# Two requests moved in a fused recurrence and router kernel: ranks one step later, a weight load behind a mask

## The chip, the cores and the metric

The kernel runs on one core of a Trainium2 chip. Its time is the device time of one execution in microseconds (us); the figure given is a median over several runs. A core has a matrix engine (PE, whose weight loads are shown as PEld), a vector engine (DVE), an activation engine (ACT), a general engine (POOL), and SP, which here only asks for transfers. Transfers (DMA) that SP asks for share one queue, q1; the indirect scatters and gathers that POOL asks for have another, q0.

## What is computed

The reference is a gated linear recurrence followed by a router with one expert for each token. The shapes are 4 batches, 8 heads, 768 positions and 48 channels a head; then 3072 tokens of 384 channels, 8 experts, 1024 hidden channels, all float32.

```python
for t in range(S):                                   # recurrence, state is D x D for each head
    state = alpha[:, :, t, :, None] * state + k[:, :, t] (x) v[:, :, t]
    y[:, :, t] = q[:, :, t] @ state
x = y as (B*S, H*D)                                  # 3072 x 384
logits = normalized(x) @ normalized(expert_emb).T / tau
e = argmax(logits);  gate = softmax(logits)[e]
out[token] = gate * (relu(x[token] @ w1[e]) @ w2[e])
```

## The kernel before

**Stage one: 24 chunks in steps.** The tokens are worked in `NS` = 24 chunks of 128 positions, 6 to a batch. A loop over `s` from 0 to 26 is a software pipeline written out by hand: step `s` works on several chunks at once. It loads chunk `s + 2` (`load`, SP: alpha in two parts, k and q; and v of chunk `s + 1`), turns chunk `s` and makes its decays (`decays`: PE transposes into `pa`, `pk`, `pq`, then a DVE scan `r` at L477 and the product `kr`; `decay_queries`: a second DVE scan `a` at L506 and the product `qs` on POOL at L510), makes the scores of chunk `s - 1` (`scores`: PE, then a mask on DVE at L577 for one half of the heads and, after a copy by ACT, on POOL by `affine_select` at L579 for the other half; that POOL instruction is kept as `st[s]["masked"]`), mixes chunk `s - 2` and turns chunk `s - 3` into rows of tokens with their logits (`rows`, L649 to L653).

The order on PE is written out: every block of matmuls stands in `with in_turn()`, which puts it behind the last matmul so far. On POOL a step's scatters stand `behind(s)`, behind the `qs` product of that step. On the other engines, SP among them, the order is that of the program except where the build puts an instruction that is ready earlier ahead of one that is not.

**Routing inside the pipeline.** The chunks are routed in groups (`GROUPS`): 0-3, 4-7, 8-11, 12-13, 14-15, 16-19, 20-22 and 23. When the last chunk of a group has its rows, `choose(g)` finds each token's expert on DVE and adds up how many tokens each expert had before each chunk (`before[:, s + 1]`, L340; on POOL, but on DVE for chunks 15 and 23). Some steps later `place(g)` makes each token's rank within its expert with two PE matmuls (three for the groups that end at chunk 15 and 23, which also need the totals), read by DVE at L362 to L369. From then on the group's chunks stand in the list `send`, and each step sends one of them, or two when more than two are waiting, to DRAM, sorted by expert: `to_rows`, an indirect scatter from POOL at L311 into `xs`.

How many steps later `place` comes is set at L690:

```python
late = 2 if s1 > NS - 3 else 3 if s1 == S0 else 4
placed_at.setdefault(s1 + late, []).append(g)
```

`s1` is the chunk after the group's last, and `S0` = 16. The group that ends at chunk 15 is therefore placed in step 19, the others in the step `s1 + 4`, but for the last two.

**The early start.** After 16 chunks at least one expert is sure to have 256 tokens. `first_expert` (DVE, L375 to L389) takes the first such expert from the totals of chunk 0 to 15 and writes the order in which the experts are worked (`turn_i`) and their first rows (`row0`). When chunk 15 has been sent, `fetch_early` (SP, L177 to L181) asks for that expert's first 256 rows out of `xs`, into `exg`; it waits for all the scatters before it. `weights(0)` (SP, L137 to L144; `w1` at L141, `w2` at L144, 1.5 MB each) is asked for in step 22, behind the last load of v. `weights(1)`, for the second expert, is asked for in step 23. From step 24 on, `turn_early` transposes the gathered rows on PE (into `pxe`, L194) and `first_layer_early` multiplies them by the first expert's `w1` (into `phe`, L191), between the last steps of stage one. All of this is in the chain `in_turn`: the rest of step 24 on PE stands behind `turn_early`.

**Stage two: the experts.** After the loop the counts of each expert are made (`counts`), rows of padding are scattered (`to_rows(pads[...], blank)`), and `fetch(0)` and `fetch(1)` ask SP for the rows of the first two experts (L170). Then the early rows go through the second layer, and the experts are worked in turn by `run(i)`, with `weights(i + 2)` and `fetch(i + 2)` asked for one iteration ahead. The first readers of the second expert's weights are `mix_first(1)` (DVE, L1009) and `mix_weights` (POOL, L979).

Of the kernel before, what the change touches and what calls it, by code (L numbers as in the profile page):

```python
# [27 lines left out]
def kernel(  # L28
# [12 lines left out]
    nc = tc.nc  # L41
# [8 lines left out]
    NS = N // P  # L50
# [15 lines left out]
    S0, EARLY = 16, 2  # L66
# [63 lines left out]
    w1_s = [consts.tile([P, KT, F], FP32, name=f"w1_{i}") for i in range(NW - 1)]  # L130
# [4 lines left out]
    def weights(i):  # L135

        e = nc.values_load(  # L137
            turn_i[0:1, i : i + 1], engines=(SP,), min_val=0, max_val=E - 1,
            skip_runtime_bounds_check_because="a sum of two experts, less E from E on",
        )  # L140
        nc.sync.dma_start(  # L141
            out=w1_s[i % NW], in_=w1_r[ds(e, 1)].rearrange("e p k f -> (e p) k f")
        )
        nc.sync.dma_start(  # L144
            out=w2_s[i % NW], in_=w2_r[ds(e, 1)].rearrange("e p k d -> (e p) k d")
        )
# [49 lines left out]
    def in_turn():  # L196
        return tc.issue_after(last["pe"].ins) if last else ExitStack()


    with ExitStack() as c1:  # L200
# [226 lines left out]
        st = [dict() for _ in range(NS)]  # L427
# [16 lines left out]
        def load(s):  # L444

            if s < NS:
                b, c = divmod(s, NCH)
                i = s % NBUF
                for p0, p1 in ((1, AROW), (AROW, P)):
                    nc.sync.dma_start(out=at_s[i][p0:p1, :, 0:D], in_=a_r[b, c, p0:p1])  # L450
                nc.sync.dma_start(out=kt_s[i][:, :, 0:D], in_=k_r[b, c])
                nc.sync.dma_start(out=qt_s[i][:, :, 0:D], in_=q_r[b, c])
            if s > 0:
                b, c = divmod(s - 1, NCH)
                return nc.sync.dma_start(out=vt_s[(s - 1) % NBV][:, :, 0:D], in_=v_r[b, c])
# [8 lines left out]
        def decays(s):  # L464

            d = st[s]
            i = s % NBUF
            L = NP * P
            pa = turned(at_s[i], "pa")
            r = r_s[s % NR]
            nc.vector.tensor_tensor_scan(  # L477
                r[:, L - 2 :: -1], pa[:, L - 1 : 0 : -1], inr[:, L - 2 :: -1],
                1.0, ALU.mult, ALU.add,
            )  # L480
            pk = turned(kt_s[i], "pk")
            d["kr"] = kr = work.tile([P, NP, P], FP32, name="kr", bufs=3)
            krf = kr.rearrange("p n t -> p (n t)")
            nc.vector.tensor_tensor(krf, pk, r, ALU.mult)
            d["pq"] = turned(qt_s[i], "pq")
            d["a"] = pa, r

        def queries(s, copied):

            d = st[s]  # L490
            d["qc"] = qc = work.tile([P, NP * P], FP32, name="qc")
            with tc.issue_after(copied.ins) if copied else ExitStack():
                nc.scalar.copy(qc, d["pq"])
# [24 lines left out]
        def keys_back(s, ps=ps_tr, tag="tr"):  # L518

            if s % NCH == NCH - 1 or "kb" in st[s]:  # L520
                return
            kr = st[s]["kr"]
            pkb = ps.tile([P, NP * P], FP32, tag=tag, name="pkb")
            for p in range(NP):
                tr(pkb[:, p * P : (p + 1) * P], kr[:, p], ident)
            st[s]["kb"] = kb = work.tile([P, NP * P], FP32, name="kb")
            nc.scalar.copy(kb, pkb)
# [135 lines left out]
        def turn_early():  # L663
            for t in range(EARLY):
                px = ps_tr.tile([P, KT, P], FP32, tag="tr", name="pxe")
                for k in range(KT):
                    tr(px[:, k], exg[:, t, k * P : (k + 1) * P], ident)
                nc.scalar.copy(exT[:, :, t * P : (t + 1) * P], px)
# [18 lines left out]
        send = []  # L687
        placed_at = {}
        for g, (_, s1) in enumerate(GROUPS):
            late = 2 if s1 > NS - 3 else 3 if s1 == S0 else 4  # L690
            placed_at.setdefault(s1 + late, []).append(g)

        def rows_of(s):
# [4 lines left out]
        def placing(s):  # L698

            n = None  # L700
            for g in placed_at.get(s, ()):
                r = GROUPS[g][1] - 1
                with in_turn():
                    n = place(g, r in (S0 - 1, NS - 1))
                if r == S0 - 1:
                    lead.append(n)
            return n
# [8 lines left out]
        for s in range(NS + 3):  # L716
            if s + 2 <= NS:
                v_last = load(s + 2)
            if s + 2 == NS:

                with tc.issue_after(v_last.ins):
                    weights(0)
            if 0 <= s - 1 < NS:
                with in_turn():
                    keys_back(s - 1)
            if s < NS:
                decays(s)
            if s == NS:
                with in_turn():
                    turn_early()  # L730
            copied = None
            if s < NS:
                placing(s)
            if 3 <= s <= NS:
                with in_turn():
                    copied = rows(s - 3)
            if s < NS:
                queries(s, copied)
                decay_queries(s)
            if 0 <= s - 1 < NS:  # L740
                decay_state(s - 1)

                with in_turn(), tc.issue_after(st[s]["a_scan"].ins) if s < NS else ExitStack():
                    scores(s - 1)
            if s == 0:
                with behind(s), in_turn():
                    prepare_first(a0)
                with behind(s):
                    prepare_logits()
            if NS <= s < NS + 2:  # L750
                with in_turn():
                    first_layer_early(2 * (s - NS), 2 * (s - NS) + 1)
            if 0 <= s - 2 < NS:
                with in_turn():
                    mix_states(s - 2)
                with in_turn():
                    mix_chunk(s - 2)
            if 0 <= s - 1 < NS:

                with in_turn(), tc.issue_after(st[s]["a_scan"].ins) if s < NS else ExitStack():  # L760
                    update(s - 1)
            if 0 < s < NS and s % NCH == 0:

                with in_turn():
                    keys_back(s, ps_mm, "mm")
            if NS <= s < NS + 2:
                with in_turn():
                    first_layer_early(2 * (s - NS) + 1, 2 * (s - NS) + 2)
            if NS <= s < NS + 2:
                with in_turn():  # L770
                    rows(s - 2)
            if s == 1:
                with in_turn():
                    turn_logits()
            if s == 2:
                with behind(s):
                    routing_constants()
            if s == 3:
                with behind(s):
                    convert_constants()  # L780
            if 4 <= s < 4 + NXG * (NC + 1):
                i, t = divmod(s - 4, NC + 1)
                with behind(s):
                    nc.gpsimd.memset(xg_s[i][:, t], 0.0)
            if s == 3:
                with behind(s):
                    nc.gpsimd.memset(blank, 0.0)

            if s >= NS:
                n = placing(s)  # L790
            if lead:
                with behind(s):
                    first_expert(lead.pop())
            with behind(s) if s < NS else tc.issue_after(st[NS - 1]["masked"].ins):
                n_now = len(send) if s >= NS else 0 if s == NS - 1 else 1 + (len(send) > 2)
                for c in send[:n_now]:
                    to_rows(dest[:, c : c + 1], x_g[group_of[c]][:, c - GROUPS[group_of[c]][0]])
                    send.remove(c)
                    if c == S0 - 1:
                        fetch_early()  # L800
            if s == NS - 1:
                weights(1)
            for r in rows_of(s):
                g = group_of[r]
                if r == GROUPS[g][1] - 1:
                    choose(g)
                    with behind(s) if s < NS else ExitStack():
                        nc.gpsimd.tensor_copy(x_g[g][:, :, TK], toks[:, slice(*GROUPS[g])])
            if s > NS:
                with in_turn():  # L810
                    first_layer_early(2 * (s - NS) + 2, 2 * (s - NS) + 4)
# [487 lines left out]
```

## Time and profile before

| | |
|---|---|
| median of 4 runs | 419.69 us (416.64 to 420.84) |
| profiled execution, its own time | 418.16 us |
| its span, first to last instruction | 416.5 us |
| busy: PE, PEld, DVE, ACT, POOL | 399.3, 354.0, 272.0, 177.7, 190.0 us |
| DMA queue q1 (SP), share of 16 engines | 49.14 MB, 50.1% |
| granted PE clock, mean | 0.996 |
| stage one, to the last matmul of `phe` | about 158 us |

A line of a timeline has the start of a run of like instructions in us from the start of the span, their time together, the engine, the line of the kernel, the operation, the tiles (written <- read), the shapes, the count, and in brackets how long the engine stood idle before it and what ended that idle time. A line of waits has the engine and what it would do, then what it waited for, and the sum, the number and the longest of these waits in us. A line of the table of windows has the window, its length, the busy time of PE, PEld, DVE, ACT and POOL with the number of instructions, the granted PE clock, the busy share of the DMA engines and GB/s. L191 and L194 are lines of helpers through which most matmuls and transposes of stage one go, so these are told apart by their tiles.

### The profile page before, as it was taken

The page shows a single profiled execution, that of the slowest core. Times are in us where ns is not written, and L with a number is a line of the kernel's source. Part 1 is how long each engine was busy: PE and PEld are TensorE (multiplying, and loading weights), DVE is VectorE, ACT ScalarE, POOL GpSimd, SP SyncE. Part 2 cuts the span into 40 slices and gives each one's busy share as a digit, 9 for nine tenths or more (in the row PEclk, how much of TensorE's full clock was granted, in tenths as well). Part 3 has the DMA queues.
Part 4 walks back from the last instruction along what each step waited for, and adds up shares of the span by engine and source line. Part 5 has one row for each costly group of instructions (what it writes and reads, how often), then busy time and mean ns, then how long its engine had stood idle before and what let it go on. Part 6 is the DMA issues. An engine that isn't in the chain of part 4 may idle for free. (4 is left out here: it accounts for less than half of the span.)

```text
span 416.5 us, 12218 instructions
## 1 busy us (share of the span) xinstructions
PE 399.3 (96%) x4730; PEld 354.0 (85%) x4730; DVE 272.0 (65%) x725; ACT 177.7 (43%) x478; POOL 190.0 (46%) x283
## 2 busy tenths in 40 slices
PE   7899999999899989999999999999999999999992
PEld 6788989889788776879799799799889979979982
DVE  7998989799798334715855945934762684684531
ACT  4455554645455426453523524522541362362310
POOL 7555586878575277308027027025203703603501
PEclk9999999999999999999999999999999999999998
DMA  9999999999998964959008119018204601001001
GB/s 140 156 162 153 156 193 181 202 169 181 195 205 221 392 221 138 308 185 350 2 35 326 67 44 352 26 52 299 76 19 162 241 2 58 2 0 55 0 18 43
DMA packets 119378, 60.25 MB, mean 145 GB/s; under 512 B 102287, under 2 KB 113816, under 8 KB 119312
## 3 DMA queue, kind: packets, MB, share of 16 engines
q1 hardware_dynamic: 115208, 49.14, 50.1%
q0 software_dynamic: 3728, 10.16, 7.0%
q8 instruction: 44, 0.72, 0.8%
q14 instruction: 22, 0.18, 0.2%
q10 hardware_dynamic: 376, 0.05, 0.1%
HBM read 49.69 MB, written 11.45 MB: 147 GB/s over the span
## 5 line engine op out<-in xcount | busy, mean ns | idle before, releaser
L850 POOL DMA_INDIRECT out_dram<-y,sx x25 | 24.3, 971 | 158.0 <-DVE gsh L906 77.4
L1032 PE MATMUL pq<-xT,w 128*128 128x192 f32 x280 | 64.5, 329 | 0.6
L955 DVE TENSOR_TENSOR hT<-pq,v 128x192 f32<-128x192 f32 x84 | 30.0, 357 | 33.5 <-PE pq L1032 31.7
L1032 PEld LDWEIGHTS pq<-xT,w 128*128 128x128 f32 x280 | 47.3, 190 | 2.8 <-DVEq L1198 1.7
L510 POOL TENSOR_TENSOR qs<-qc,a 128x512 f32<-128x512 f32 x24 | 30.6, 1276 | 34.9 <-DVE a L506 23.7
L939 PE MATMUL pyo<-w,hT 128*128 128x384 f32 x128 | 43.3, 492 | 0.0
L939 PEld LDWEIGHTS pyo<-w,hT 128*128 128x128 f32 x128 | 23.8, 190 | 15.3
L1032 PE MATMUL pq<-xT_m,w_m 128*128 128x192 f32 x168 | 36.5, 326 | 0.0
L1040 ACT ACTIVATE hT<-hT 128x384 f32<-128x384 f32 (+1 forms) x56 | 24.8, 443 | 23.0 <-DVE hT L955 19.9
L477 DVE TENSOR_TENSOR_SCAN r<-pa,inr 128x511 f32<-128x511 f32 x24 | 29.1, 1215 | 6.7 <-PE pa L194 6.5
L506 DVE TENSOR_TENSOR_SCAN a<-pa,ini 128x512 f32<-128x512 f32 x24 | 29.3, 1222 | 1.0
L1080 PE MATMUL pq<-w_m,hT_m 128*128 128x192 f32 x168 | 29.6, 326 | 0.0
L311 POOL DMA_INDIRECT xs<-x,dest x24 | 24.2, 1009 | 11.3 <-DVE x L653 6.2
L979 POOL TENSOR_TENSOR w_m<-w 128x384 f32<-128x384 f32 x28 | 27.4, 998 | 3.7 <-DMA out_dram<-y,sx 2.7
L1032 PEld LDWEIGHTS pq<-xT_m,w_m 128*128 128x128 f32 x168 | 28.9, 190 | 0.0
L1040 ACT ACTIVATE hT<-pq 128x192 f32<-128x192 f32 x28 | 9.2, 330 | 43.5 <-PE pq L1032 43.5
L1080 PEld LDWEIGHTS pq<-w_m,hT_m 128*128 128x128 f32 x168 | 27.7, 190 | 0.0
L979 POOL TENSOR_TENSOR w_m<-w,w_m 128x384 f32<-128x384 f32 x28 | 27.1, 996 | 0.0
L191 PE MATMUL sc<-qs,kr 64*64 64x128 f32 x768 | 26.3, 271 | 0.5 <-issue 0.5
L191 PE MATMUL pyx<-sm,vt 128*64 128x128 f32 x384 | 26.7, 279 | 0.0
L955 DVE TENSOR_TENSOR v<-pq,v 128x192 f32<-128x192 f32 x56 | 20.0, 356 | 8.4 <-ACT v L1043 5.2
L1087 DVE SCALAR_TENSOR_TENSOR y<-pq,gt,u 128x192 f32<-128x192 f32 x21 | 8.8, 418 | 24.6 <-PE pq L1080 24.6
(203 smaller groups left out, 932.0 us busy)
## 6 DMA issues: line engine op xcount, KB each, us to landing
w<-in_moe_w_dram SPq DMA_DIRECT2D x16, 1536.0 KB, 7.7
kt<-in_k_dram SPq DMA_DIRECT2D x24, 192.0 KB, 3.8
qt<-in_q_dram SPq DMA_DIRECT2D x24, 192.0 KB, 5.7
vt<-in_v_dram SPq DMA_DIRECT2D x24, 192.0 KB, 5.5
xg<-xs SPq DMA_DIRECT2D x22, 196.5 KB, 7.1
at<-in_alpha_dram SPq DMA_DIRECT2D x24, 168.0 KB, 5.2
xg<-xs SPq DMA_DIRECT2D x8, 98.2 KB
at<-in_alpha_dram SPq DMA_DIRECT2D x24, 22.5 KB, 4.3
```

What stands on the lines that cost most here:

```text
L191: last["pe"] = nc.tensor.matmul(*args, **kwargs)
L311: ins = nc.gpsimd.indirect_dma_start(out=xs, out_offset=bass.IndirectOffsetOnAxis(ap=rows, axis=0), in_=x, in_offset=None, bounds_check=E ...
L477: nc.vector.tensor_tensor_scan(r[:, L - 2 :: -1], pa[:, L - 1 : 0 : -1], inr[:, L - 2 :: -1], 1.0, ALU.mult, ALU.add,)
L506: d["a_scan"] = by_dve = nc.vector.tensor_tensor_scan(a, pa, ini, 0.0, ALU.mult, ALU.add)
L510: by_pool = nc.gpsimd.tensor_tensor(qs.rearrange("p n t -> p (n t)"), d["qc"], a, ALU.mult)
L850: ins = nc.gpsimd.indirect_dma_start(out=out, out_offset=bass.IndirectOffsetOnAxis(ap=col, axis=0), in_=y, in_offset=None, bounds_check=N - 1,
L939: pe[:] = [nc.tensor.matmul(py, lhsT=hT[:, f], rhs=w2_t[:, f], start=(f == 0), stop=(f == FT - 1),)]
L955: dve[:] = [call(*args)]
L979: nc.gpsimd.tensor_tensor(to[:, f], x[:, f], y[:, f], ALU.subtract)
L1032: pe[:] = [nc.tensor.matmul(to, lhsT=left, rhs=right, start=start, stop=stop, skip_group_check=True,)]
L1040: return nc.scalar.activation(h, p, AF.Relu)
L1080: pe[:] = [nc.tensor.matmul(to, lhsT=left[:, f], rhs=right[:, f], start=start and f == 0, stop=stop and f == n - 1, skip_group_check=True,)]
```

## The change

The group of chunks 14 and 15 loses its special case and is placed in step 20 instead of 19. With it move its two scatters in the list `send`, `first_expert`, and `fetch_early`, which follows chunk 15's scatter: that goes out in step 21 instead of 20.

`weights(1)` is written in step 24 instead of 23. Ahead of it one column of its `w1` tile is set to zero on POOL, behind the mask of the last chunk; the load of `w1` overwrites that column and so has to wait for it.

```diff
@@ -687,7 +687,7 @@
         send = []
         placed_at = {}
         for g, (_, s1) in enumerate(GROUPS):
-            late = 2 if s1 > NS - 3 else 3 if s1 == S0 else 4
+            late = 2 if s1 > NS - 3 else 4
             placed_at.setdefault(s1 + late, []).append(g)
 
         def rows_of(s):
@@ -798,7 +798,9 @@
                     send.remove(c)
                     if c == S0 - 1:
                         fetch_early()
-            if s == NS - 1:
+            if s == NS:
+                with tc.issue_after(st[NS - 1]["masked"].ins):
+                    nc.gpsimd.memset(w1_s[1][:, 0, 0:1], 0.0)
                 weights(1)
             for r in rows_of(s):
                 g = group_of[r]
```

## The prediction

> **What bounds the kernel now.** I read the page first: the busy shares, then the chain that ended last.
>
> ```profile
> PE 399.3 (96%) x4730; PEld 354.0 (85%) x4730; DVE 272.0 (65%) x725; ACT 177.7 (43%) x478; POOL 190.0 (46%) x283
> ```
>
> PE is busy for 399.3 of 416.5 us: a delay of PE anywhere is a delay of the end, because nothing behind it has spare time, and a gain is worth what PE waits less. The diff touches steps 19 to 24 (about 106 to 143 us). The waits from 104 to 124 us, longest first:
>
> ```profile
> DVE before L340 <- POOL before L340: 2.0, 1, 2.0
> ...
> PE pyx L191 <- POOL before L340: 1.5, 1, 1.5
> ...
> PE pq L194 <- DMA qt<-in_q_dram: 0.5, 1, 0.5
> ```
>
> They sit in step 19. From one step's first transpose (of `pa`) to the next one's is 5.3 us, but 8.5 us from step 19 to step 20 (105.98 to 114.52). PE stops at the rank matmuls; the timeline of PE has them, and the two places of step 24 that matter below:
>
> ```profile
> 109.67 0.40 PE L191 MATMUL pyx<-before,ones 128*128 128x16 f32 x2 [1.52 <-POOL before L340]
> ...
> 136.24 0.87 PE L194 MATMUL pxe<-ident,xg 128*128 128x128 f32 x6
> ...
> 139.44 1.56 PE L191 MATMUL phe<-exT,w 128*128 128x256 f32 x6
> ```
>
> `pxe` is the first reader of the early rows (the gather, `fetch_early`), `phe` of the first expert's `w1`. DVE's timeline over the same steps shows who really holds step 19:
>
> ```profile
> 109.65 0.17 DVE L340 TENSOR_TENSOR before<-before,chosen 128x8 f32<-128x8 f32 x1 [2.04 <-POOL before L340]
> 109.73 1.21 DVE L477 TENSOR_TENSOR_SCAN r<-pa,inr 128x511 f32<-128x511 f32 x1
> ...
> 125.39 0.42 DVE L560 TENSOR_TENSOR state<-pd,dec 128x256 f32<-128x256 f32 x1 [0.18 <-PE pd L191]
> 126.33 1.22 DVE L477 TENSOR_TENSOR_SCAN r<-pa,inr 128x511 f32<-128x511 f32 x1 [0.52 <-PE pa L194]
> ```
>
> DVE stands 2.04 us in its own addition at L340, which `choose` makes in step 18 and the change leaves there. Step 19's scan starts right behind it. From 109.73 to 122.3 DVE has no gap.
>
> Last, SP's queue, which asks for the gather and the weights, and POOL, whose scatters the gather waits for:
>
> ```profile
> 124.03 3.18 SPq L455 DMA_DIRECT2D vt<-in_v_dram  x2
> 128.62 0.40 SPq L181 DMA_DIRECT2D xg<-xs  x1
> 129.55 1.31 SPq L141 DMA_DIRECT2D w<-in_moe_w_dram  x1
> 131.04 0.37 SPq L144 DMA_DIRECT2D w<-in_moe_w_dram  x1
> 131.92 1.84 SPq L141 DMA_DIRECT2D w<-in_moe_w_dram  x1
> ```
>
> ```profile
> 121.67 1.01 POOL L311 DMA_INDIRECT xs<-x,dest  x1 [0.15 <-issue]
> ...
> 124.59 1.28 POOL L510 TENSOR_TENSOR qs<-qc,a 128x512 f32<-128x512 f32 x1 [0.52 <-DVE a L506]
> ```
>
> The scatter at 121.67 is chunk 15's, the last that the gather needs; the list of DMA issues gives it 4.3 us to landing (126.0). SP is busy with the loads until 127.21 and asks for the gather at 128.62, so today the gather isn't late. `fetch_early` is written in step 20, ahead of the loads that end at 127.21, yet stands behind them: the build lets SP's transfers that are ready sooner go first.
>
> **The change part by part.** *Ranks in step 20.* The matmuls (0.77 us of PE, 109.67 to 110.44), three DVE operations at L362 to L369 (0.2 us each at most) and `first_expert` (L375 to L389, about 2.1 us of DVE, 113.45 to 115.42 and 0.3 more) go one step on; nothing is saved. PE's 1.52 us wait goes, as the ranks' operands are then long there. What is late next is DVE: behind its 2.04 us it has the same operations to do between 109.73 and the scan of step 21 at 121.09, in another order and without a gap, so that scan does not move. What can shrink are DVE's later waits for a PE that is now ahead, 0.18 and 0.52 us. Bounds 0 to 0.7 us; with step 21's transposes of PE some 0.9 us earlier, and PE held again by the `a` scan whose bank it reuses, I take a gain of 0.4 at `pxe`: 135.8.
>
> *Scatters of chunks 14 and 15, and the gather.* `send` now holds 13 in step 19, 14 in step 20 and 15 in step 21: three scatters as before, one a step, about 1 us of POOL each, hidden in POOL's idle 1 to 2 us a step. Chunk 15's follows the `qs` product of 124.59, at 125.9, and lands 4.3 to 5.1 us later (chunk 15 and chunk 14 of today), at 130.3 to 131.1. SP is free at 127.21 and can't ask for the gather before then. The weights of the first expert need only `turn_i` (some 120 us) and the last load before them. If SP takes them first, it asks for `w1` 0.55 us after 127.21 (as it takes 0.53 us from the gather's issue to `w1`'s today), at 127.75, which is 1.8 us sooner than 129.55. The packets of the trace run through this one queue in the order asked: the gather's rows until 131.75, `w1` until 136.7, `w2` until 140.7. 1.8 us sooner, `w2` ends at 138.9. Then the gather's 0.40 MB: 1.0 us at the 401 to 422 GB/s of the windows from 133 to 136 us, or 2.2 us as it took on its own, and up to 0.7 us from last packet to landing (131.75 to 132.43). It lands at 140.3 to 141.6; I take 141.0. PE's order is chained by hand, so everything of step 24 stands behind `pxe`: 141.0 instead of 136.24 is **+4.8 us** (4.1 to 5.4), the 0.4 swallowed.
>
> *The clock behind such a gap.* PE would be idle 5.2 us, and no gap of this trace after the start is over 1.52 us. The nearest rows are at its ends. The last matmul ends at 409.1:
>
> ```profile
> 412.00:413.00 1.00, 0.00 (x0) 0.00 (x0) 0.00 (x0) 0.00 (x0) 0.00 (x0) 1.00 0.32 120
> 413.00:414.00 1.00, 0.00 (x0) 0.00 (x0) 0.00 (x0) 0.00 (x0) 0.00 (x0) 0.53 0.03 5
> ```
>
> The granted clock falls to half 4.0 us after it; and at the start a group of four transposes takes 1.06 us until 6.9 us, 5.3 us behind the first matmul (1.55), and 0.6 us later. So the price is between 0 (no fall) and 2.65 us (half of 5.3); I take **1.0**, as part of slower matmuls hides in the waits of ACT and DVE in that step.
>
> [...]
>
> *Second expert's weights behind the mask.* New is a memset of 128x1 on POOL; the nearest rows are 0.43 us (128x393, L784) and 0.21 (an addition of 128x8), so 0 to 0.43, taken 0.2. Its place is behind the mask at 140.26, where POOL idles 5.13 us: it costs nothing, or 0.2 if it stood behind the four scatters at 146 to 151, where PE waits 1.06 us for POOL. Its `w1` DMA then waits on SP; behind it stand `w2` and the fetches, of which the first goes at 160.75, so 15 us are free. Today these weights are asked for at 131.92 and 133.94, but their packets start at 140.3, behind the first expert's: moving the request to 141 (or 146 with the late gather) moves the data little. They would land by 150 to 158; their first reader is at 169.85 (DVE, L1009). Price 0.
>
> **The sum** against the profiled execution's 418.16 us (span 416.5): +4.8 +1.0 = 424.0. The median of the runs is 419.69, 1.53 above that execution, so **425.5**; own range 423.4 to 427.7.
>
> **Rivals**, on the scale of the median. (1) *The gather keeps its place ahead of the weights.* For it: SP has it there now. Against: now it is ready when SP comes free, then 3 to 4 us later. SP would stand until 130.3 to 131.1; the gather, 3.8 us from issue to landing (128.62 to 132.43), is there by 135, in time. `w1` is asked for 0.9 us behind it, lands 7.7 us later at 139.0 to 139.9, and `phe` wants it at 139.0: 0 to 0.9 us of new wait against the 0.4 gained. 419.7 (419.0 to 420.3). (2) *Between `w1` and `w2`.* `w1` ends at 134.9, the gather lands at 136.3 to 137.6 against 135.8: +0.1 to +1.4 over today, 420.3. (3) *Faster: step 19 falls to a normal step.* If the build puts DVE's addition at L340 behind step 19's scan, since its result is now needed a step later, the 2.04 us go too: all 3.2 us of excess, 416.5, and 415.0 if the waits at 138.7 (0.45) and 151 (1.06) go with weights that come later. Against: `choose` is not moved and its addition has long been written ahead of that scan. It decides only if the gather isn't late as well. (4) *The memset lands behind the scatters*: weights and scatters share the engines until 160, the fetches are late; PE has 4 us between the rows' transposes (163.7) and the first reader (168.7): +0 to 2 us.
>
> **How the numbers follow.** Late gather 0.58, kept place 0.27, between 0.06, faster 0.06, the rest 0.03. The likeliest gives 425.5. The range takes in (1) down to 418.7 (its gain of 0.7 and no new wait, rounded out) and the late gather up to 427.7. One per cent (415.5 to 423.9), about what a measurement of this kernel can tell from no change, parts the cases: faster 0.04, mostly (3); within 0.43, which is (1), (2), half of (3) and the late gather with a short tail and no fall of the clock (0.05); slower 0.53.
>
> **What would show it.** Right: L181 behind the first L141 and L144 in SP's timeline; `pxe` at about 141 with a wait of some 5 us for DMA xg; a granted clock under 1.0 just after; no wait of PE at the ranks, but DVE's 2.0 us at L340 still there. Wrong: L181 ahead of L141, and `pxe` before 137; or step 19 to 20 under 6 us.

## The result, and the profile after

The changed kernel takes 418.45 us (median of 42 runs, 416.03 to 421.5) against 419.38 us for the kernel before in the same set (63 runs). The ratio is **0.9974, 95% interval 0.9959 to 0.9988**: about 1.1 us faster, where 425.5 was forecast, in a range of 418.7 to 427.7. From here on every kernel is compared with the kernel before on its own chip, since on one of the chips the kernel before takes 428.59 us, 2% more than here, and the changed one 425.61.

The profiled execution of the changed kernel took 420.55 us (span 418.8), longer than its median. Where its milestones stand late, that is partly that execution, and the text says which part. Lines that stand behind L801 in the file have numbers 2 higher than in the kernel before.

SP's timeline is the first thing to read, because the forecast hung on its order (start, us, line, what is asked for):

```profile
123.31 3.11 SPq L455 DMA_DIRECT2D vt<-in_v_dram  x2
130.15 0.40 SPq L181 DMA_DIRECT2D xg<-xs  x1
131.08 0.38 SPq L141 DMA_DIRECT2D w<-in_moe_w_dram  x1
131.64 0.37 SPq L144 DMA_DIRECT2D w<-in_moe_w_dram  x1
142.36 0.37 SPq L141 DMA_DIRECT2D w<-in_moe_w_dram  x1
```

The gather (L181) is still ahead of the first expert's weights (L141, L144). SP is free at 126.42 and stands until 130.15, for chunk 15's scatter, which landed at 129.94. The gather landed at 133.16, `w1` at 139.66. Last line: the second expert's `w1` is asked for behind the memset. POOL's timeline has that scatter and the memset:

```profile
126.60 1.01 POOL L311 DMA_INDIRECT xs<-x,dest  x1 [0.15 <-issue]
...
142.23 0.10 POOL L803 MEMSET w<- 128x1 f32 x1
```

PE's timeline, at the places shown of before (in brackets: how long PE stood idle before it, and for what):

```profile
114.58 0.29 PE L191 MATMUL pyx<-before,ones 128*128 128x16 f32 x2
...
121.81 0.26 PE L191 MATMUL px<-sel,ycols 64*64 64x56 f32 x1 [1.34 <-DVE state L560]
...
136.27 0.88 PE L194 MATMUL pxe<-ident,xg 128*128 128x128 f32 x6
...
140.53 0.38 PE L191 MATMUL sc<-qs,kr 64*64 64x128 f32 x2 [1.76 <-issue]
140.84 1.54 PE L191 MATMUL phe<-exT,w 128*128 128x256 f32 x4
```

The 1.52 us at the ranks are gone, though PE now stands 0.93 and 0.69 us for DVE in step 19 (`pkb` and `pa`). What is won comes back as 1.34 us at `px<-sel`, two steps later, so `pxe` starts at 136.27 as it did before (136.24). Step by step: from the first transpose of step 19 to that of step 20 it is 7.18 us instead of 8.54, the next step takes 5.51 instead of 5.83, and the one after it 7.00 instead of 5.35. DVE's timeline shows who holds step 21:

```profile
118.45 0.80 DVE L381 TENSOR_SCALAR turn_f<-cols,lead 128x8 f32<-128x8 f32 x1
...
119.69 0.67 DVE L385 CAST turn_i<-turn_f 1x8 int32<-1x8 f32 x1
...
121.33 0.42 DVE L560 TENSOR_TENSOR state<-pd,dec 128x256 f32<-128x256 f32 x1
```

The chain of `first_expert` (L375 to L389) now runs in step 21, between 117.9 and 121.4, and `state`, for which PE waits, stands behind it. One link of it is longer than it was. The cast at L385 takes 0.67 us here; the line of before is

```profile
115.26 0.16 DVE L385 CAST turn_i<-turn_f 1x8 int32<-1x8 f32 x1
```

It takes 0.67 to 0.69 us in all eight profiles here that have the ranks late and chunk 15's scatter one step behind chunk 14's, and 0.16 in the other nine. In the eight, POOL's mask follows the scatter that runs beside the cast, in the nine a second scatter does; what holds the cast is not shown. Ahead of the chain, DVE still stands 2.0 us in its own addition:

```profile
DVE before L340 <- POOL before L340: 2.0, 1, 2.0
...
PE px L191 <- DVE state L560: 1.3, 1, 1.3
...
PE pkb L194 <- DVE kr L484: 0.9, 1, 0.9
```

(These are waits from 104 to 124 us: what waits, for what, sum, number, longest.) In this execution `phe` is 1.40 us later than before, mostly because of the 1.76 us ahead of the score matmuls (0.45 before). Right behind that gap, the table of windows (window, length, busy us of PE, PEld, DVE, ACT, POOL, granted clock, DMA share, GB/s) has a stretch of half clock:

```profile
141.40:144.80 3.40, 3.40 (x27) 2.25 (x27) 0.00 (x0) 0.57 (x2) 0.68 (x2) 0.50 0.67 168
```

From the first group of `phe` to the second it is 4.68 us instead of 3.12: the stretch cost 1.56 us. So 1.40 + 1.56 = 2.96 us of this execution's lateness lie in step 24.

### The profile page after: what moved, and what is told of

Its sections match the earlier page's. It is cut to its first block, busy times and chain, and to the rows that moved or that the text cites. A ratio compares the mean times of both kernels' runs of the same rounds, so it can differ in the third digit from the quotient of the medians.

```text
span 418.8 us, 12218 instructions
## 1 busy us (share of the span) xinstructions
PE 400.3 (96%) x4730; PEld 356.1 (85%) x4730; DVE 271.3 (65%) x725; ACT 178.1 (43%) x478; POOL 190.3 (45%) x284
```

## The experiments

**The parts on their own.** Four kernels on the slower chip, where the kernel before takes 428.59 us: the kernel before itself, the first part, the second part, and both.

```diff
-            late = 2 if s1 > NS - 3 else 3 if s1 == S0 else 4     # first part: ranks_alone
+            late = 2 if s1 > NS - 3 else 4
...
-            if s == NS - 1:                                       # second part: weights_alone
+            if s == NS:
+                with tc.issue_after(st[NS - 1]["masked"].ins):
+                    nc.gpsimd.memset(w1_s[1][:, 0, 0:1], 0.0)
                 weights(1)
```

> The kernel of before once more, for a second profile and for the granted clock of each of its runs. Theory A (the gain is in the granted clock): its runs fall into groups by the mean granted clock, each 3.4 us at half clock costs some 1.5 to 2 us, and before has more such stretches than the changed kernel (over 0.7 a run, as against about 0.7 for the changed one by its own list of runs). Theory B (the gain is work that PE does sooner, the same in every run): as many stretches as the changed kernel, and at an equal clock before is about 1 us slower. Either way 419.4 us and ratio 1.00.

Measured: 428.9 us, ratio 1.0014 (0.9983 to 1.0045). That is the noise of one such set.

> Only the ranks are moved; the second expert's weights are asked for as before. Theory B, with the gain from the ranks: 418.3, ratio 0.997. If the gain comes from the later weights: 419.4, ratio 1.00. In the profile the transposes of step 20 come about 1.4 us sooner than in before and those of step 22 at the same time, because DVE has to catch up in step 21; the gather is asked for ahead of the first expert's weights, at about 130.

Measured: 425.04 us, 0.9931 (0.9903 to 0.9958).

> Only the second expert's weights are asked for later, behind the memset and the mask; the ranks stay in step 19. If the gain comes from the ranks: 419.4, ratio 1.00, with PE's wait of 1.5 us at the ranks back. If it comes from the later weights: 418.3, ratio 0.997. The recorded view (moving that request moves the data little, price 0) expects no difference.

Measured: 426.83 us, 0.9959 (0.9930 to 0.9988).

> The changed kernel once more: 418.3 us, ratio 0.997. A second profile tells whether the wait of 1.8 us ahead of the last score matmuls of step 24 and the 3.4 us at half clock behind it belong to the kernel or to that one execution: if to the kernel, both are there again; if to the execution, the wait is near 0.5 us as in before and the clock stays at 1.0 from 12 us to the end.

Measured: 425.61 us, 0.9962 (0.9936 to 0.9988).

Each part gains here, and both together gain no more than the first: the parts don't add. In these profiles PE stands 2.13 us at the ranks without the first part and 1.2 us at `px<-sel` with it. The gap ahead of the score matmuls is there in all four (1.22 to 1.41 us, and a second one of 1.68 in the kernel before), so it is not the change's doing. Of theory A (the gain is in the granted clock): the mean clock of the runs is 0.989 before, 0.993 with the first part, 0.991 with both. From run to run in this set, 0.01 of clock goes with 2.2 us, so 0.004 more clock is an estimated 0.9 us; with the first part 0.7% was measured, 3.0 us, so the clock alone does not explain it.

The same two, later, on a chip where the kernel before takes 418.95 us:

> The change's first line alone (the ranks one step later; the second expert's weights stay where they were), on another chip than the first time, where it measured 0.993. Theory A, the ranks themselves gain on PE: again 0.993 to 0.995. Theory B, what PE wins in step 19 it stands again in step 21 (px<-sel, 1.2 to 1.3 us) and at the instructions of step 24 or at phe, and the 0.993 belongs to the first chip, where PE's wait at the ranks was 2.1 us and not 1.5: 0.996 to 0.999 here.

Measured: 418.49 us, 1.0002 (0.9970 to 1.0034). The waits of PE from 98 to 160 us:

```profile
PE px L191 <- DVE state L560: 1.4, 1, 1.4
...
PE sc L191 <- issue: 1.0, 1, 1.0
PE phe L191 <- DMA w<-in_moe_w_dram: 0.9, 1, 0.9
```

The ratio lies just above theory B's range, and the waits are theory B's, all its takers in one list: DVE's chain, the gap of step 24, and `w1`, which is asked for at 132.34 and lands at 141.08.

> The change's second part alone (the memset behind the last mask and the second expert's weights behind it), on another chip than the first time, where it measured 0.996. Theory A, nothing on PE's path waits for these transfers or stands behind them: 0.999 to 1.001. [...]

Measured: 419.08 us, 0.9994 (0.9961 to 1.0028): theory A on this chip. Why both parts gained on the slower chip and neither on this one stays open. The profiles of the slower chip show two differences. One is PE's longer wait at the ranks, which weights_alone_2 has here as well (2.22 us). The other is a wait in stage two, the only one of PE from 164 to 185 us:

```profile
PE pq L927 <- DVE xT L879: 2.0, 1, 2.0
```

The line is from unchanged. The wait (1.97 us; 12 matmuls of `pq` behind it take 2.16 and 2.44 us, 1.50 in the profile of before) is in both kernels of that chip that have the ranks in step 19, unchanged and weights_alone, in neither that has them late, and not in the profiles of before and of the changed kernel. If the slower matmuls are a stretch of half clock, and it costs the 1.56 us of the one above, that is an estimated 3.5 us, as much as the 0.7% of the first part; why the ranks' step should matter there is open, and it is one profile of each.

**The forecast order, forced.** Four kernels on a third chip, the kernel before at 418.92 us: this pair, and the first two of the next part. First the changed kernel once more, as their neighbour:

> The changed kernel once more, beside the other three of this set. 0.996 to 0.997 of the kernel before, as on the two chips so far. The recorded view should show a wait of 2.0 us on DVE ahead of its addition L340 (released by POOL's addition of the chunk before) and a wait of 1.2 to 1.3 us on PE at px<-sel, two steps later.

Measured: 418.84 us, 0.9984 (0.9951 to 1.0016); DVE's 2.0 us and PE's 1.35 us at `px<-sel` are both there. `w1` landed at 141.34, `phe` began at 141.47.

```diff
                 with tc.issue_after(v_last.ins):
                     weights(0)
+                fetch_early()
...
-                    if c == S0 - 1:
-                        fetch_early()
```

> The changed kernel with one line moved: the gather of the first expert's rows (L181) is traced behind the two requests for that expert's weights (L141, L144), so that SP takes them in the order that the prediction had assumed. Theory A, the prediction's price holds once the order is forced: SP asks for w1 and w2 near 127, some 4 us sooner than in the changed kernel (131.1 and 131.6), the gather's packets stand behind them in the queue and land at 139 to 141 instead of 133.2, the first transpose of the gathered rows (pxe) starts near 140.5 instead of 136.3, and the kernel is 4.1 to 5.4 us slower than the changed one, with 0 to 2.7 more if the granted clock falls behind the gap: 1.009 to 1.017 of the kernel before on this chip. Theory B, the gather's small packets do not wait for the weights that were asked before them, or the wait lies where PE waits anyway: landing by 135, pxe within 1 us of the changed kernel, ratio 0.995 to 0.999.

Measured: 422.91 us, 1.0096 (1.0059 to 1.0134), 4.1 us over the changed kernel beside it by the medians, and 4.7 by the ratios (1.0096 less 0.9984, of 419). **Theory A.** SP's and PE's timelines:

```profile
125.67 1.76 SPq L141 DMA_DIRECT2D w<-in_moe_w_dram  x1
127.94 0.39 SPq L144 DMA_DIRECT2D w<-in_moe_w_dram  x1
130.30 0.37 SPq L181 DMA_DIRECT2D xg<-xs  x1
```

```profile
135.79 0.54 PE L191 MATMUL sc<-qs,kr 64*64 64x128 f32 x9 [1.75 <-issue]
140.72 1.51 PE L194 MATMUL pxe<-ident,xg 128*128 128x128 f32 x6 [1.20 <-DMA xg<-xs]
```

The gather lands at 140.58, 10.3 us after it is asked for instead of 3.0, and `pxe` starts at 140.72, 4.6 us later than in the changed kernel beside it. Only 1.20 us of that show as a wait for the gather, because PE had already been held in step 23 by a gap of 1.75 us for nothing that the profile shows, and its matmuls ran slower behind that gap (16 of `pyx<-sm,vt` at 136.81 in 1.86 us, 1.09 in send_both). Without these two it would have stood longer at the same landing. SP asked for `w1` at 125.67, 2.1 us sooner than the prediction had it, and `w1` took 9.9 us to land instead of 7.7, so that the landing agrees with the forecast is in part luck.

**What takes the gain back: DVE or the late scatter.** Chunk 14's addition on DVE, in the changed kernel and in the kernel before:

```diff
-                eng = nc.vector if s in (S0 - 1, NS - 1) else nc.gpsimd
+                eng = nc.vector if s in (S0 - 2, S0 - 1, NS - 1) else nc.gpsimd
```

> The changed kernel with chunk 14's addition before<-before,chosen (L340) made on DVE, as chunk 15's is, instead of on POOL, where it stands behind two scatters and a mask. Theory A, the change's gain on PE is given back because DVE stands 2.0 us for POOL's addition and then brings the chain of the turn (L362 to L395) late into step 21: with the wait gone, PE's 1.2 to 1.3 us at px<-sel go too, pxe starts 0.5 to 1.3 us sooner, and the ratio falls from 0.996 to 0.993 or 0.994. Theory B, the time that DVE spends on the chain itself (some 3.3 us of small instructions in step 21) makes PE wait wherever it stands: DVE's wait goes, PE's at px<-sel stays over 0.8 us, and the ratio stays at 0.996 to 0.997.

Measured: 418.92 us, 1.0002 (0.9971 to 1.0032). DVE's wait is gone, PE's at `px<-sel` is 1.15 us: of the waits theory B is right, the chain costs PE its time wherever DVE's wait stands; the ratio is neither's. What neither theory had is the next line of PE's timeline:

```profile
141.96 2.47 PE L191 MATMUL phe<-exT,w 128*128 128x256 f32 x5 [3.61 <-DMA w<-in_moe_w_dram]
```

Chunk 15's scatter landed at 131.83, so `w1` was asked for at 132.97 and landed at 141.82. POOL had started that scatter at 126.18, no later than in the changed kernel (126.60); it took 5.65 us to land instead of 3.34. That is one execution, and the landing of this scatter takes between 3.3 and 5.7 us in these profiles.

> The kernel before with chunk 14's addition on DVE: the ranks stay in step 19. Theory A, PE's 1.5 to 2.1 us wait at the ranks (pyx<-before,ones) is for POOL's late addition alone: the wait goes without moving the ranks, and the ratio is 0.995 to 0.997, like the change's. Theory B, the ranks come too soon in step 19 whoever adds: DVE's own addition is then the last to end, PE's wait stays over 0.8 us, and the ratio is 0.999 to 1.001.

Measured: 416.89 us, 0.9946 (0.9914 to 0.9979), at the edge of theory A's range. PE's waits from 104 to 124 us are down to two, and `pxe` starts at 134.06:

```profile
PE px L191 <- DVE state L558: 0.7, 1, 0.7
PE pyx L191 <- DVE n L369: 0.3, 1, 0.3
```

So the ranks were not too early in step 19: POOL's addition, queued behind two scatters and a mask, was too late. Nothing has to move.

The order between the two, on top of dve_adds (`w1`, gather, `w2`):

```diff
                 with tc.issue_after(v_last.ins):
-                    weights(0)
+                    weights(0, (0,))        # w1 alone
+                fetch_early()
+                weights(0, (1,))            # w2
...
-                    if c == S0 - 1:
-                        fetch_early()
```

> The changed kernel with chunk 14's addition on DVE (as in the run before it) and one order more changed on SP: the first expert's first weights (L141) are asked for ahead of the gather (L181), the second ones (L144) behind it. Theory A, what the later ranks give back is the gather's and the weights' lateness: chunk 15's scatter lands at 130 to 132, SP stands for it, w1 is asked for at 131 to 133 and lands 8 to 9 us later, at 139.7 to 141.8, while PE could begin phe at 138.3. With w1 asked for near 127.5 it lands by 137, the gather lands behind it by 136.5, PE's 3.6 us wait at phe becomes under 1 us, and the ratio falls from 1.000 to between 0.990 and 0.994. Theory B, PE waits there for something else, or the gather behind w1 comes as late as in the run with both weights ahead (140.6): a wait of over 2 us stands at pxe or phe, and the ratio stays over 0.998.

Measured: 417.36 us, 0.9952 (0.9921 to 0.9982). Inconclusive: the wait for `w1` is gone (landed 138.06), but the gather behind it landed at 139.09 and PE stood 2.64 us at `pxe`, as theory B had it; the ratio lies between the two theories.

The next edit leaves the program of DVE alone and only sends chunk 15's scatter with chunk 14's (of the line, only the end that changes is shown in full):

```diff
-                n_now = len(send) if s >= NS else 0 if s == NS - 1 else 1 + (len(send) > 2)
+                n_now = ... else 1 + (len(send) > 2 or S0 - 1 in send)
```

> The changed kernel, with POOL sending chunk 15's scatter right behind chunk 14's in step 20 instead of one step later (in step 22 by the trace, 126.4). Theory A, the change gives its gain back through the lateness of scatter, gather and weights: chunk 15's scatter lands near 124.5, SP no longer stands for it (1.4 to 3.7 us until now), the gather is asked for near 127 to 128, w1 lands by 137 instead of 139.7 to 141.8, PE's phe no longer waits for it, and the ratio falls by 0.3 to 0.6 per cent, to between 0.992 and 0.995. [...]

Measured: 416.97 us against 419.76, 0.9944 (0.9917 to 0.9972). The ratio is theory A's, and so are the transfers: the scatter landed at 125.17, SP no longer stands for it, `w1` landed at 137.35:

```profile
127.56 0.40 SPq L181 DMA_DIRECT2D xg<-xs  x1
128.49 0.38 SPq L141 DMA_DIRECT2D w<-in_moe_w_dram  x1
```

```profile
139.26 0.38 PE L191 MATMUL sc<-qs,kr 64*64 64x128 f32 x2 [0.93 <-issue]
139.56 1.56 PE L191 MATMUL phe<-exT,w 128*128 128x256 f32 x6
```

`phe` is 1.28 us sooner than in the changed kernel's profile, and no half clock follows (the first and the second group of `phe` take 1.56 us each, the mean clock is 0.997). But that `phe` had waited for `w1` is not shown: in the changed kernel it started 1.2 us after `w1` had landed, behind the gap ahead of the score matmuls, and that gap is 0.93 here instead of 1.76. Nor did DVE stay as it was:

```profile
119.76 0.16 DVE L385 CAST turn_i<-turn_f 1x8 int32<-1x8 f32 x1
```

```profile
121.38 0.26 PE L191 MATMUL px<-sel,ycols 64*64 64x56 f32 x1 [0.83 <-DVE state L560]
```

The cast at L385 is short again, PE's wait for `state` is 0.83 us instead of 1.34, and `pxe` is 0.44 us sooner. So beside the earlier scatter and its transfers three things differ (the cast, the gap and the clock), and this run does not part them. Against the changed kernel (0.9974, 0.9984 and, on the slower chip, 0.9962) the gain is 0.2 to 0.4 per cent; the intervals overlap, so the size is an estimate and the direction rests on the traces as well.

**Better versions.** The kernel before, with DVE also adding for chunks 20 to 22, whose ranks PE had waited 1.05 us for (in the set with the kernel before at 418.95 us, as w1_first):

```diff
-                eng = nc.vector if s in (S0 - 1, NS - 1) else nc.gpsimd
+                eng = nc.vector if s in (S0 - 2, S0 - 1) or s >= NS - 4 else nc.gpsimd
```

> The kernel before with DVE making the additions L340 of chunk 14 and of chunks 20 to 22 as well; POOL makes the others. In the run with chunk 14 alone PE stood 1.05 us at the ranks of chunks 20 to 22 (149.11 to 150.16), for POOL's three additions behind four scatters, while DVE was idle. Theory A, that wait is on the path: it goes, and the ratio falls from 0.995 to 0.992 or 0.993, with chunk 14's part as before. Theory B, what follows (the scatters on POOL, one each 1.28 us, up to the first rows of the next expert) ends last whatever PE does: PE's wait goes and comes back at the next layer, ratio 0.994 to 0.996.

Measured: 415.91 us, 0.9932 (0.9897 to 0.9967). PE's wait is gone and the two groups of `phe` around it stand 2.58 us apart instead of 3.70; theory A, though its interval overlaps that of dve_adds_b. The same additions on send_both, and the change's second part on dve_adds_c:

> The kernel of the run before it, with DVE making the additions L340 of chunks 14 and 20 to 22. Theory A: with the lateness gone, DVE's 2.0 us wait and PE's 1.05 us at the ranks of chunks 20 to 22 are worth what they are worth in the kernel before: 0.989 to 0.993. Theory B: PE's wait at px<-sel in step 21 (1.1 to 1.4 us) stays, being DVE's chain itself, and the best with the ranks late stays behind the best with the ranks in step 19: 0.993 to 0.996.

Measured: 415.37 us, 0.9920 (0.9886 to 0.9954). Theory A.

> The kernel before with DVE's additions for chunks 14 and 20 to 22 (0.993 in the run of it), and with the change's second part on top: the second expert's weights behind a memset behind the last mask. Theory A, the weights' request is not on the path: 0.993 again, within 0.002. [...]

Measured: 415.15 us, 0.9898 (0.9863 to 0.9934), from 6 runs. The ratio is 0.001 under theory A's range of 0.991 to 0.995, and its interval reaches into that range. In the profile PE's gap ahead of the scores is 2.37 us and `w1` landed at 139.01, against 2.17 and 140.34 in dve_adds_c. The gap is no shorter, and 1.0 of the 1.3 us by which `w1` is sooner were there at the start of step 19 (105.43 against 106.43), before either request. What the second part is worth stays open. Either kernel beats both that the study began with: 0.8 and 1.0% under the kernel before.

The milestones in one place (us; all but the first two rows are from the three chips at 419 to 420 us; one profiled execution each). The first column is the first transpose of step 19: where it differs, that much of the other columns was there before the edits act.

| kernel | step 19 | scatter 15 landed | gather asked | `w1` landed | `pxe` | `phe` |
|---|---|---|---|---|---|---|
| before | 105.98 | 125.94 | 128.62 | 137.21 | 136.24 | 139.44 |
| changed | 106.03 | 129.94 | 130.15 | 139.66 | 136.27 | 140.84 |
| both_third | 105.93 | 130.16 | 130.37 | 141.34 | 136.10 | 141.47 |
| gather_late | 105.61 | 130.10 | 130.30 | 135.59 | 140.72 | 144.41 |
| dve_adds | 106.46 | 131.83 | 132.05 | 141.82 | 135.84 | 141.96 |
| w1_first | 107.13 | 131.96 | 132.16 | 138.06 | 139.22 | 142.98 |
| send_both | 106.12 | 125.17 | 127.56 | 137.35 | 135.83 | 139.56 |
| dve_adds_b | 105.55 | 124.54 | 126.99 | 136.87 | 134.06 | 138.14 |
| send_both_adds | 106.02 | 122.96 | 126.58 | 136.49 | 134.00 | 138.08 |

## Why the prediction was wrong, point by point

**The step that failed** is in the part on the scatters and the gather: "If SP takes them first, it asks for `w1`" sooner, and with it the chance of 0.58 for the late gather. SP did not take them first. What happened is the first rival, "the gather keeps its place ahead of the weights", which had 0.27 and 419.7 (419.0 to 420.3) beside it. Its steps were nearly met: SP stood until 130.15 (forecast 130.3 to 131.1), the gather was there at 133.16 (by 135), `w1` was asked for 0.93 us behind it and landed at 139.66 (139.0 to 139.9). Its time was not: 418.45 lies 0.2 to 0.5 us under its range, as one takes the kernel before at 419.38 or at the prediction's 419.69.

The premise came from one observation, that the gather is written in step 20 and stands behind loads of later steps; from this I took "the build lets SP's transfers that are ready sooner go first" and applied it to the weights, with ready times read from the trace. In the changed kernel the gather is written in step 21 and the weights in step 22, and that order stood, although by the trace the gather is ready 3.5 us later (129.94 against 126.42). That the build moved it past one neighbour did not show that it would move it past the next; by what rule the build kept this order is not shown. Forced, the order costs about what was worked out: landing 140.58 (140.3 to 141.6), `pxe` 140.72 (141.0), 4.0 us over the kernel before, where the sum had 5.8 with the clock and its range began at 3.7. So it was the condition that was wrong more than its price. (The range of the landing does not come out of its terms: 138.9 with 1.0 to 2.2 and 0 to 0.7 on it gives 139.9 to 141.8. Nothing hangs on it.)

**Ranks, forecast gain 0.4 at `pxe`** (0 to 0.7): 0.0 in the changed kernel's profile, 0.1 in both_third. The text said that DVE has the same operations to do "in another order and without a gap, so that scan does not move". The scan of step 21 moved from 121.09 to 121.67. The order is not what moved it: 0.51 of the 0.58 us are the cast at L385 (0.67 for 0.16). In send_both, where the cast is short and the order the same, that scan comes 11.36 us behind the scan of step 19, exactly as before, and `pxe` starts at 135.83, the forecast's 135.8. So what this term lacked is a cast that is longer in one place than in another, which no row of before showed. That DVE's 2.04 us at L340 would stay is right, and that they would be *the* taker is not: with them gone (dve_adds) PE still stood 1.15 us, though `pxe` came 0.9 us sooner, counted from step 19.

**New wait at `phe`, 0 to 0.9 us in the first rival**: 0.94 in ranks_alone_2, 3.61 in dve_adds, none beyond the gap ahead of the scores in the changed kernel, 0.17 in both_third. So the mechanism was right there, and its upper end too low: where the scatter lands at 131.8 instead of 130.3 to 131.1, `w1` lands at 141.82.

**The clock** was priced only for a gap of 5.2 us. It fell behind a gap of 1.76 us, and cost 1.56 us in that execution. In other profiles PE's matmuls ran slower behind gaps of 1.75 (gather_late) and 2.37 us (adds_c_weights), and not behind one of 2.17 (dve_adds_c).

**Memset and second weights, price 0**: 0.10 us in POOL's idle time at 142.23, ahead of the scatters; second weights landed at 148.9 and 153.1 (forecast 150 to 158). weights_alone_2 at 0.9994 agrees; the slower chip, at 0.9959, does not, and that is open.

**Where the small gain of 0.3% lies** is not settled. The profile pair shows 1.36 + 0.32 us won in steps 19 and 20 and 1.65 given back in step 21, of which 0.51 are the cast. send_both shows what more the change could have had with that scatter a step sooner.

The clock is a rival for all of these small gains. On the chips at 419 to 420 us the runs of the kernel before have a mean granted clock of 0.991 to 0.992, those of the changed kernel 0.994 (0.992 in both_third), dve_adds_b 0.995, send_both 0.995; for the kernel before beside the changed one no clocks are on record. Within the four later sets, 0.01 of clock goes with 2.2 to 2.5 us from run to run. By this estimate the kernels differ from the one before, at an equal clock, by -1.3 us (dve_adds_b), -1.2 (send_both), -1.9 (dve_adds_c), -3.3 (send_both_adds), -3.2 (adds_c_weights), -0.2 (both_third) and +0.7 (dve_adds), each give or take 1.0 to 1.2. What gained keeps more than half of its gain. Of the change itself nothing clear is left there, while on the slower chip it keeps -1.7. Whether its clock is better because it has one long gap of PE fewer is not shown.

## What to carry to other kernels

When a wait is moved instead of removed, follow every consumer of the moved result to its last reader. Here the ranks cost nothing a step later, but the scatter, the gather, the weights and PE's first layer all stand behind them (in gather_late, with `w1` and `w2` asked for ahead of it, the gather landed 10.3 us after it was asked for instead of 3.0). Ask first who is late: a 0.2 us addition queued behind two scatters and a mask on POOL held DVE for 2.0 us and PE for 1.5 to 2.2, and giving it to DVE gained 0.5%, where moving its reader gained 0.3 (the intervals overlap). And a transfer order that a build chooses is a condition with its own odds. Both orders were priced here; the one that was picked rested on a single observation.

## What the runs showed of the hardware that was not expected

In the changed kernel's profile the granted clock fell to half for 3.4 us behind a gap of PE of 1.76 us (141.40 to 144.80, clock 0.50). Matmuls ran slower behind other single gaps too: behind 1.75 us in gather_late (16 matmuls `pyx<-sm,vt` in 1.86 us, 1.09 in send_both), behind 1.97 us in unchanged and weights_alone (12 matmuls of `pq` in 2.16 and 2.44 us, 1.50 before), and behind 2.37 us in adds_c_weights (the first six of `phe` in 2.23 us, 1.56 before). Behind 2.17 us in dve_adds_c the same six took 1.53 us, behind 1.28 us in send_both_adds 1.56; and in the kernel before, whose gap at the ranks is 1.52 us, the clock was 1.00 from 6.9 us to the last matmul. From the first group of `phe` to the second it is 4.68 us in the changed kernel and 4.67 in adds_c_weights, against 3.08 to 3.12 in before, send_both, send_both_adds and dve_adds_c.

The length of a gap does not part these cases (2.17 us without slower matmuls, 1.75 with them), and what does is not shown. Nor does every execution of one kernel pay for it: the mean clock of the changed kernel's 42 runs lies between 0.986 and 0.999. 3.4 us at half clock take an estimated 0.004 off the mean clock of a run of 417 us, so a run at 0.999 has no room for such a stretch, and the 1.56 us of the profiled execution (0.987) are not a fixed price of the kernel.

PE's gap ahead of the score matmuls of step 24, "for nothing that the profile shows", was 0.45 us before, 1.76 in the changed kernel, 0.93 in send_both, 1.27 in dve_adds_b, 1.28 in send_both_adds, 2.17 in dve_adds_c and 2.37 in adds_c_weights; gather_late has 1.75 in step 23. Each figure is from one execution, and what PE stands for there is not shown.
